# Sparse attention and mixture of experts on one core: mask products moved a step ahead, value products regrouped, GpSimd's indirect DMAs released at other places

## Chip, cores and metric

One core of a Trainium2 chip. The metric is the device time of one launch in microseconds (us). It is given as the median of several runs. A profile is one further execution, taken by the hardware profiler.

## The reference

The input is q, k and v of shape (8 batches, 8 heads, 576 positions, 64 columns), all float32. Heads 0 to 3 attend locally: position i sees positions i-31 to i. Heads 4 to 7 attend with a stride: position i sees the earlier positions that have the same remainder by 32. The outputs of all heads, laid side by side, are 4608 tokens of 512 columns. A router (a 512 by 8 product, plus a bias that depends on the token's modality) picks the best of eight experts for each token, and the token goes through that expert's two layers (512 to 1024, relu, 1024 to 512), scaled by the softmax weight of the pick:

```python
logits = x @ w_gate + modality_bias[modality_id]
e_idx = argmax(logits); gate_w = softmax(logits)[e_idx]
out[mask_e] = gate_w * (relu(x[mask_e] @ w1[e]) @ w2[e])
```

## The kernel before

**Stages.** The kernel has an attention stage and an expert stage, and TensorE (PE) runs through both without a barrier. The attention stage works in 32 *units*, two heads or two batches at a time: 16 local ones (class `Local`) and 16 strided ones (class `Strided`), alternating. Four local and four strided units make a *pair of batches*; its tokens are put in rows, routed, ranked within their expert and scattered to a list in device memory (`finish_pair`, `route`, `scatters`). The expert stage takes slots of 256 tokens from that list and runs them through `ffn`; the first slots start while the last pair of batches is still being routed.

**A unit's steps.** `load` and `load_values` issue its DMAs on the sync engine's queue (SP). `scores` adds the scores to a mask: first a *mask product*, an identity matrix (128 rows by 128 columns of PE's array) times a constant mask of 0 and -2^30, which opens the PSUM bank (L341 for the two halves of a local unit, L434 for a strided one); then many small products on top of it: eight and eight of 128 rows by 32 columns of the array (L345), four more of the same form (L352); for a strided unit 32 of 128 rows by 18 columns (L438). VectorE (DVE) takes the maximum and subtracts it, ScalarE (ACT) takes the exponential. `turn` transposes the result on PE (L208; `t` for a local unit, `ts` for a strided one) and ACT or DVE copies it to SBUF. `values` multiplies by v: a local unit has 16 products of 64 columns of the array (L390), eight into one bank and eight into another, and four of 32 columns and 64 rows (L401) between them; a strided unit has 16 of 64 columns (L482, tile `ot`). DVE then divides a local unit's rows by their sums (L406 to L408), and ACT copies a strided unit's (L490).

**What sets the order.** The order on PE is the order in which the code issues it. The loop at L1005 has one step per unit: step n issues the loads of unit n+3, the value loads of unit n-1, the scores of unit n, two pieces of leftover work (`pop(MIDS)`, pieces of `finish_pair` and `route`), `turn` of unit n-2, one `slow()`, `values` of unit n-3, three more pieces, and one more `slow()`. The order on the other engines is made by a scheduler, except where `pin` holds an instruction to the program's order. PSUM has eight banks, which all PE outputs share in turn.

**Releases.** GpSimd (POOL) issues the indirect DMAs: nine scatters of 128 token rows per pair of batches (L608), and, before the expert stage, the first weights (`raw`, L773) and tokens (`fx`, L754). Each call of `slow()` issues one of them, and `paced` makes it wait for the PE instruction that the list `recent` holds at that moment: the last transpose, or the last value product, that the code has issued. So the first `slow()` of a step waits for the transposes of `turn`, and the second for the last value product, or for a transpose that a leftover piece has put behind it.

**Setup for the router.** `routing_setup` (L227) runs once, in step 6: five small loads on SP, then two DVE instructions (L237, L239) and three GpSimd ones (L248 to L250) that make the bias of all tokens.

Of the kernel before, what the change touches and what calls it, by code (L numbers as in the profile page):

```python
# [14 lines left out]
I32 = mybir.dt.int32  # L15
# [6 lines left out]
B, H, S, D = 8, 8, 576, 64  # L22
# [4 lines left out]
DM = H * D  # L27
# [6 lines left out]
NSTATIC = 18  # L34
ROW = DM + 16
WARM = 10
SETUP = 6
POPS, MIDS, POPF = 5, 2, 2
LT, RK = 7, (10, 5)
LAG = 2  # L40
# [15 lines left out]
M_L = M_ID + P  # L56
M_S = M_L + 9 * 64
# [127 lines left out]
def attention_moe(ctx: ExitStack, tc: tile.TileContext, a, out):  # L185
    nc = tc.nc
# [6 lines left out]
    def pa(name):  # L193
        return ps.tile([P, 512], F32, tag="a", name=name)
# [10 lines left out]
    recent = []  # L205
# [21 lines left out]
    def routing_setup():  # L227

        pin(nc.sync.dma_start(wg.rearrange("p c e -> p (c e)"), a["wg"]))
        modi = cp.tile([P, 36], I32, name="modi")  # L230
        pin(nc.sync.dma_start(modi[:], a["mod"]))
        mb = cp.tile([P, 2, E], F32, name="mb_sb")
        pin(nc.sync.dma_start(mb.rearrange("p m e -> p (m e)"), a["mb"]))
        pin(nc.sync.dma_start(tok[:], a["tok"]))
        pin(nc.sync.dma_start(xd[NT:NT + 1, :], a["nul"]))
        modf = cp.tile([P, 36], F32, name="modf")
        pin(nc.vector.tensor_copy(modf[:], modi[:]))  # L237
        nmod = cp.tile([P, 36], F32, name="nmod")
        pin(nc.vector.tensor_scalar(nmod[:], modf[:], -1.0, 1.0, ALU.mult, ALU.add))  # L239
        bias0 = pools["lp"].tile([P, 36, E], F32, bufs=1, name="bias0")  # L240

        def bc_e(t):
            return t.unsqueeze(2).to_broadcast([P, 36, E])

        def bc_t(t):
            return t.unsqueeze(1).to_broadcast([P, 36, E])

        pin(nc.gpsimd.tensor_tensor(bias[:], bc_e(modf), bc_t(mb[:, 1, :]), ALU.mult))  # L248
        pin(nc.gpsimd.tensor_tensor(bias0[:], bc_e(nmod), bc_t(mb[:, 0, :]), ALU.mult))
        pin(nc.gpsimd.tensor_tensor(bias[:], bias[:], bias0[:], ALU.add))  # L250

# [62 lines left out]
    class Local:  # L314
# [10 lines left out]
        def load_values(self):  # L325
# [6 lines left out]
            if n < 2:  # L332
                pin(ins)

        def scores(self):
            n, q, kd = self.n, self.qk[:, 0, 19:37, :], self.qk[:, :, 0:19, :]
            self.ex = ex = lp.tile([P, 9, 64], F32, tag="ex", name=f"ex{n}")
            for half in range(2):
                gn = 4 + half
                sp = pa(f"s{n}{half}")[:, :64 * gn]  # L340
                nc.tensor.matmul(sp, identb, cb[:, M_L + 256 * half:M_L + 256 * half + 64 * gn], start=True, stop=True)  # L341
                for m in range(2):
                    for u in range(4):
                        i = _place(2 * half + m, u)
                        nc.tensor.matmul(  # L345
                            sp[32 * u:32 * u + 32, 128 * m:128 * m + 128], q[:, i, :], kd[:, :, i:i + 2, :],
                            start=False, stop=True, skip_group_check=True,
                        )
                if half:
                    for u in range(4):  # L350
                        i = 16 + u // 2
                        nc.tensor.matmul(  # L352
                            sp[32 * u:32 * u + 32, 256:320], q[:, i, :],
                            kd[:, u % 2, i:i + 2, :].rearrange("p i q -> p (i q)"),
                            start=False, stop=True, skip_group_check=True,
                        )
# [25 lines left out]

        def values(self):
            n, et, e8, vv, xt, h = self.n, self.et, self.e8, self.vv, self.xt, self.h
            for bb in range(2):
                gn = 5 - bb
                o = pa(f"o{n}{bb}")[:, :(D + 1) * gn].rearrange("p (g c) -> p g c", g=gn)
                for k in range(4):
                    for jj in range(2):
                        recent[:] = [nc.tensor.matmul(  # L390
                            o[64 * jj:64 * jj + 64, k, :],
                            et[:, 2 * (k // 2) + bb, 2 * (k % 2) + jj, :, :].rearrange("p g q -> p (g q)"),
                            vv[:, 4 * k + 2 * jj + bb, :],
                            start=True, stop=True, skip_group_check=True,
                        )]
                if bb == 0:
                    for jj in range(2):
                        for b2 in range(2):
                            r0 = 64 * b2 + 32 * jj
                            u = 2 * jj + b2  # L400
                            nc.tensor.matmul(  # L401
                                o[r0:r0 + 32, 4, :], e8[:, 32 * u:32 * u + 32], vv[0:64, 16 + u, :],
                                start=True, stop=True, skip_group_check=True,
                            )
                rs = lp.tile([P, 5], F32, tag="rs", name=f"rs{n}{bb}")
                nc.vector.tensor_scalar(rs[:, :gn], o[:, :, D], 1e-9, None, ALU.add)  # L406
                nc.vector.reciprocal(rs[:, :gn], rs[:, :gn])
                nc.vector.tensor_tensor(  # L408
                    xt[:, 5 * bb:5 * bb + gn, D * h:D * h + D], o[:, :, 0:D],
                    rs[:, :gn].unsqueeze(2).to_broadcast([P, gn, D]), ALU.mult,  # L410
                )

    class Strided:

# [9 lines left out]
        def load_values(self):  # L424
# [3 lines left out]
            if n < 2:  # L428
                pin(ins)

        def scores(self):
            n, qk = self.n, self.qk
            s = pa(f"ss{n}")[:, :288]
            nc.tensor.matmul(s, identb, cb[:, M_S:M_S + 288], start=True, stop=True)  # L434
            for i in range(8):
                for u in range(4):
                    r = 16 * (i // 4) + 4 * u + i % 4
                    nc.tensor.matmul(  # L438
                        s[32 * u:32 * u + 18, 36 * i:36 * i + 36], qk[:, 32 + r, :], qk[:, r:r + 65:64, :],
                        start=False, stop=True, skip_group_check=True,  # L440
                    )
            s3 = s.rearrange("p (i k) -> p i k", i=16)

            def bc(t):
# [82 lines left out]
    def route(bp, xt, xcs):  # L527
# [59 lines left out]
        nc.vector.tensor_reduce(sm[:], lo[:], AX.X, ALU.add)  # L587
        nc.vector.tensor_scalar(sm[:], sm[:], 1e-9, None, ALU.add)
        nc.gpsimd.memset(xt[:, :, DM + 2:ROW], 0.0)
        nc.vector.tensor_copy(xt[:, :, DM].bitcast(I32), tok[:, 9 * bp:9 * bp + 9])  # L590
        nc.vector.reciprocal(xt[:, :, DM + 1], sm[:])

        for _ in range(RK[bp == NBP - 1]):
# [368 lines left out]
    def slow():  # L962
        while calm and next(calm[0], calm) is calm:
            calm.pop(0)
# [3 lines left out]
    def pop(k):  # L968
        for _ in range(k):
            while extra and next(extra[0], extra) is extra:  # L970
                extra.pop(0)
# [30 lines left out]
        units[i].load()  # L1002
    man = tc.manual_schedule(engines={mybir.EngineType.PE})
    man.__enter__()
    for n in range(nu + 3):  # L1005
        if n + 3 < nu:
            units[n + 3].load()
        if 1 <= n <= nu:
            units[n - 1].load_values()
        if n < nu:  # L1010
            units[n].scores()
            pop(MIDS)
        if 2 <= n <= nu + 1:
            units[n - 2].turn()
        slow()
        if n >= 3:
            units[n - 3].values()
            if n - 3 in ends:
                extra.append(after(*ends[n - 3]))
        if n == SETUP:  # L1020
            routing_setup()
        pop(POPS - MIDS if n < nu else POPS)
        slow()
        if n == nu + 1:
            turn(0)
    while calm:
# [71 lines left out]
```

## Time and profile before

| what | value |
|---|---|
| median of 3 runs | 596.82 us (595.97 to 598.28) |
| the profiled execution | 594.6 us |
| its span, first to last instruction | 592.8 us |
| PE busy | 568.4 us, 96% of the span |
| DVE, ACT, GpSimd busy | 72%, 60%, 38% |
| HBM traffic | 241 GB/s over the span |

The times of an instruction are its start and its length. PE's products overlap, and their ends are modelled, so the time that a run of products holds PE is read from its start to the start of the next run, not from its length. A product of float32 operands shows as two records, so that eight products read "x16". "128\*32" in a PE row is the part of the array that it uses, rows by columns. A gap ahead of an instruction stands in brackets with what ended it; "issue" means that the profile shows nothing that it waited for. The DMA share is the mean busy share of the core's 16 DMA engines. In section 3 of the page, "instruction" queues are those by which the engines' own instructions are fetched.

### The profile page before, as it was taken

To read this page: it belongs to the slowest core of one execution; us is meant where nothing else is said; L and a number is where in the kernel's file an instruction comes from. 1 tells how busy PE (TensorE), PEld (TensorE's weight loads), DVE (VectorE), ACT (ScalarE), POOL (GpSimd) and SP (SyncE) were. 2 spreads that over 40 slices of the span, in tenths; PEclk is the share of its full clock that TensorE was granted. 3 is DMA by queue.
4 is the path that set the end of the run, shared out by engine and by line. 5 is a ranking of instruction groups with operands and counts; after the bars stand their busy time and mean duration, and the time that the engine had idled before them with its cause. 6 is when DMAs were issued, how large, how long until landed. Compare 5 with 4: busy or idle time off the path is not lost.

```text
span 592.8 us, 15232 instructions
## 1 busy us (share of the span) xinstructions
PE 568.4 (96%) x6040; PEld 491.0 (83%) x6040; DVE 425.2 (72%) x1082; ACT 358.5 (60%) x739; POOL 227.9 (38%) x201
## 2 busy tenths in 40 slices
PE   7888998898999999999999999999999999999995
PEld 4666776676887999999999999999998998999984
DVE  6556674957969997867867767777777777677542
ACT  3345765656866566666666666666665676666642
POOL 1010041233666786652542533533534533332310
PEclk9789999999999999999999999999999999999999
DMA  8998698996798855964934932413504438200721
GB/s 275 289 263 258 201 346 268 297 352 223 261 219 212 267 147 174 245 187 108 276 102 124 214 138 64 108 38 73 108 28 81 109 127 247 70 14 25 241 97 39
DMA packets 66670, 102.50 MB, mean 173 GB/s; under 512 B 47327, under 2 KB 48607, under 8 KB 63008
## 3 DMA queue, kind: packets, MB, share of 16 engines
q0 software_dynamic: 19744, 58.57, 29.9%
q1 hardware_dynamic: 46560, 42.48, 28.3%
q8 instruction: 49, 0.80, 0.6%
q10 hardware_dynamic: 288, 0.41, 0.3%
q14 instruction: 29, 0.24, 0.1%
HBM read 123.66 MB, written 19.43 MB: 241 GB/s over the span
## 4 chain that ended last, share of the span: by engine, by line
PE 90%; issue 5%; DVE 2%; DMA 1%; ACT 1%; POOL 0%; POOLq 0%; ACTq 0%
PE h L886 35%; PE o L900 34%; PE o L390 3%; PE s L345 3%; PE ot L482 3%; PE ss L438 2%; PE t L208 2%; PE xl L208 1%; PE ts L208 1%; PE xs L208 1%; PE s L341 1%; PE lg L533 1%; DMA lqk<-in_qkl 1%; PE o L401 1%; DMA xd<-xt,posi 1%
## 5 line engine op out<-in xcount | busy, mean ns | idle before, releaser
L922 DVE TENSOR_TENSOR wl<-raw,wh 128x512 fp32r<-128x512 f32 x288 | 186.2, 685 | 85.1 <-ACT wh L921 83.8
L921 ACT CAST wh<-raw 128x512 fp32r<-128x512 f32 x288 | 164.2, 619 | 90.6 <-PE o L900 90.5
L886 PE MATMUL h<-xl,wh 128*128 128x256 f32 x576 | 162.0, 282 | 1.1 <-DVE xl L874 1.1
L886 PE MATMUL h<-xh,wl 128*128 128x256 f32 x576 | 163.0, 284 | 0.0
L886 PE MATMUL h<-xh,wh 128*128 128x256 f32 x576 | 162.6, 284 | 0.2 <-ACT xh L873 0.2
L773 POOL DMA_INDIRECT raw<-in_w,wi x72 | 90.9, 1263 | 166.7 <-DVE wl L922 154.1
L886 PEld LDWEIGHTS h<-xl,wh 128*128 128x128 f32 x576 | 108.7, 189 | 7.6 <-DVE xl L874 1.3
L900 PE MATMUL o<-wh,hh 128*128 128x512 f32 x288 | 114.5, 398 | 0.0
L886 PEld LDWEIGHTS h<-xh,wh 128*128 128x128 f32 x576 | 108.4, 189 | 6.7 <-ACT xh L873 0.6
L900 PE MATMUL o<-wl,hh 128*128 128x512 f32 x288 | 113.6, 394 | 0.0
L900 PE MATMUL o<-wh,hl 128*128 128x512 f32 x288 | 112.3, 395 | 0.0
L886 PEld LDWEIGHTS h<-xh,wl 128*128 128x128 f32 x576 | 108.3, 188 | 0.9
L889 ACT ACTIVATE hh<-h 128x256 fp32r<-128x256 f32 x144 | 55.4, 385 | 54.7 <-PE h L886 52.7
L608 POOL DMA_INDIRECT xd<-xt,posi x36 | 40.4, 1122 | 83.9 <-DVE xt L408 50.4
L891 DVE SCALAR_TENSOR_TENSOR hl<-h,hh 128x256 fp32r<-128x256 f32 x144 | 60.1, 418 | 12.0 <-ACT hh L889 12.0
L900 PEld LDWEIGHTS o<-wh,hl 128*128 128x128 f32 x288 | 53.7, 188 | 11.7
L900 PEld LDWEIGHTS o<-wh,hh 128*128 128x128 f32 x288 | 54.3, 188 | 7.7
L900 PEld LDWEIGHTS o<-wl,hh 128*128 128x128 f32 x288 | 54.3, 189 | 5.9
L908 POOL DMA_INDIRECT out<-y,le x36 | 46.0, 1278 | 24.6 <-ACT y L907 17.4
L754 POOL DMA_INDIRECT fx<-xd,li x36 | 39.2, 1088 | 23.5 <-issue 11.9
L379 ACT COPY et<-t 64x512 f32<-64x512 f32 x32 | 18.6, 580 | 29.3 <-PE t L208 28.9
L907 ACT ACTIVATE y<-o,le 128x512 f32<-128x512 f32 x36 | 24.6, 689 | 4.3 <-PE o L900 4.2
(180 smaller groups left out, 673.1 us busy)
## 6 DMA issues: line engine op xcount, KB each, us to landing
lqk<-in_qkl SPq DMA_DIRECT2D x32, 296.0 KB
sqk<-in_qks SPq DMA_DIRECT2D x32, 288.0 KB
vv<-in_vl SPq DMA_DIRECT2D x16, 520.0 KB
vs<-in_vs SPq DMA_DIRECT2D x16, 288.0 KB
raw<-in_w,wi POOLq DMA_INDIRECT x72, 4.9
vv<-in_vl SPq DMA_DIRECT2D x16, 65.0 KB
xd<-xt,posi POOLq DMA_INDIRECT x36, 5.8
fx<-xd,li POOLq DMA_INDIRECT x36, 4.5
```

The source lines that it names most:

```text
L208: recent[:] = [nc.tensor.transpose(dst, src, ident)]
L608: scattered(bp, paced(nc.gpsimd.indirect_dma_start(xd[0:(bp + 1) * T2, :], IOA(ap=posi[:, i:i + 1], axis=0), xt[:, i, :], None)))
L754: yield xt, fetches(min(xrows // T2, NBP) - 1, nc.gpsimd.indirect_dma_start(xt[:, h, :], None, xd[0:xrows, :], IOA(ap=li[:, s, h:h + 1], a ...
L773: return nc.gpsimd.indirect_dma_start(raws[j].rearrange("p f c -> p (f c)"), None, a["w"], IOA(ap=wi[:, s, j:j + 1], axis=0), bounds_check ...
L886: recent[:] = [nc.tensor.matmul(hp, w[:, a1], x[:, c, :], start=(k == 0), stop=(k == 11))]
L889: nc.scalar.activation(hh[:], hp, AF.Relu)
L891: nc.vector.scalar_tensor_tensor(hl[:], hp, 0.0, hh.bitcast(F32), ALU.max, ALU.subtract)
L900: nc.tensor.matmul(os[h], hx[:, m], w[:, 512:1024], start=(f == 0 and i == 0), stop=(f == 7 and i == 2))
L907: nc.scalar.mul(y[:], os[h], gate[:, h:h + 1])
L908: outs.add(nc.gpsimd.indirect_dma_start(out, IOA(ap=le[:, h, 0:1], axis=0), y[:], None, bounds_check=NT - 1, oob_is_err=False))
L921: nc.scalar.copy(wh[:, c], raw[:, c])
L922: nc.vector.tensor_tensor(wl[:, c], raw[:, c], wh[:, c].bitcast(F32), ALU.subtract)
```

## The change

The change has five parts.

1. Each class has a new method `masks`, with the mask products that stood at the head of `scores`. The loop calls it one step ahead: unit 0's before the loop, unit n+1's in step n behind `turn` and the first `slow()`, ahead of `values` of unit n-3.
2. In a local unit's `values`, the eight products of the first bank come first, then the eight of the second, then the four of 32 columns, which now go to the second bank. So the first bank has 4 groups and the second 5, and the rows land where they did.
3. A strided unit's last score product is put in `recent`, and the place of a step's second `slow()` moves: in an odd step (scores of a strided unit) one `slow()` comes right behind `scores`, and the last one ahead of the leftover pieces rather than behind them; an even step has only the `slow()` behind `turn`. Two steps together still have four.
4. `routing_setup` is now in two parts: its loads stay in step 6, its arithmetic goes to step 9, and its first DVE instruction is `paced`.
5. The copy of the token numbers (L590) is `paced` as well.

```diff
-SETUP = 6
+SETUP = 6, 9
...
         pin(nc.sync.dma_start(xd[NT:NT + 1, :], a["nul"]))
+        yield
...
-        pin(nc.vector.tensor_copy(modf[:], modi[:]))
+        pin(paced(nc.vector.tensor_copy(modf[:], modi[:])))
...
+        def masks(self):
+            self.sp = []
+            for half in range(2):
+                gn = 4 + half
+                sp = pa(f"s{self.n}{half}")[:, :64 * gn]
+                nc.tensor.matmul(sp, identb, cb[:, M_L + 256 * half:M_L + 256 * half + 64 * gn], start=True, stop=True)
+                self.sp.append(sp)
...
-            for half in range(2):
+            for half, sp in enumerate(self.sp):
...
+            blocks(0)
+            normed(0)
+            blocks(1)
+            ends()
+            normed(1)
...
+        def masks(self):
+            self.s = pa(f"ss{self.n}")[:, :288]
+            nc.tensor.matmul(self.s, identb, cb[:, M_S:M_S + 288], start=True, stop=True)
...
-                    nc.tensor.matmul(
+                    recent[:] = [nc.tensor.matmul(
                         s[32 * u:32 * u + 18, 36 * i:36 * i + 36], qk[:, 32 + r, :], qk[:, r:r + 65:64, :],
...
-        nc.vector.tensor_copy(xt[:, :, DM].bitcast(I32), tok[:, 9 * bp:9 * bp + 9])
+        paced(nc.vector.tensor_copy(xt[:, :, DM].bitcast(I32), tok[:, 9 * bp:9 * bp + 9]))
...
+    units[0].masks()
+    setup = routing_setup()
     for n in range(nu + 3):
...
             units[n].scores()
+            if n % 2:
+                slow()
             pop(MIDS)
         if 2 <= n <= nu + 1:
             units[n - 2].turn()
         slow()
+        if n + 1 < nu:
+            units[n + 1].masks()
         if n >= 3:
             units[n - 3].values()
             if n - 3 in ends:
                 extra.append(after(*ends[n - 3]))
-        if n == SETUP:
-            routing_setup()
+        if n in SETUP:
+            next(setup)
+        if n >= nu or n % 2:
+            slow()
         pop(POPS - MIDS if n < nu else POPS)
-        slow()
```

**The order on PE, local half of two steps.** Before, from the transposes of a strided unit (`ts2`) through the value products of a local unit (`o20`, `o21`: its two banks) to the scores of the next local unit (`s40`, `s41`: its two halves):

```order
L208 MATMUL ts2_661<-cf_sb_65,ens2_486 72x128 x4
L390 MATMUL o20_670<-vv2_440,et0_88 64x65 x8
L401 MATMUL o20_670<-vv2_440,e82_574 32x65 x4
L390 MATMUL o21_687<-vv2_440,et0_88 64x65 x8
L341 LDWEIGHTS cb_sb_63
L341 MATMUL s40_705<-cb_sb_63 128x256
L345 MATMUL s40_705<-lqk0_84 32x128 x8
L341 LDWEIGHTS cb_sb_63
L341 MATMUL s41_719<-cb_sb_63 128x320
L345 MATMUL s41_719<-lqk0_84 32x128 x8
L352 MATMUL s41_719<-lqk0_84 32x64 x4
```

The same place now (the line numbers are those of the changed file: L342 is the mask, L398 and L410 the value products, L353 and L360 the scores):

```order
L208 MATMUL ts2_653<-cf_sb_65,ens2_486 72x128 x4
L342 LDWEIGHTS cb_sb_63
L342 MATMUL s40_662<-cb_sb_63 128x256
L342 LDWEIGHTS cb_sb_63
L342 MATMUL s41_664<-cb_sb_63 128x320
L398 MATMUL o20_666<-vv2_442,et0_88 64x65 x8
L398 MATMUL o21_667<-vv2_442,et0_88 64x65 x8
L410 MATMUL o21_667<-vv2_442,e82_574 32x65 x4
L353 MATMUL s40_662<-lqk0_84 32x128 x8
L353 MATMUL s41_664<-lqk0_84 32x128 x8
L360 MATMUL s41_664<-lqk0_84 32x64 x4
```

The two masks stand together behind the transposes, the value products run 64, 64, 32 columns rather than 64, 32, 64, and the two halves of the scores follow each other with nothing between.

**The order on PE, strided half.** Before, from the transposes of a local unit (`t13`, `t23`) through the value products of a strided unit (`ot20`, `ot21`) to a strided unit's scores (`ss4`):

```order
L208 MATMUL t13_738<-cf_sb_65,ex3_531 128x128 x4
L208 MATMUL t23_743<-cf_sb_65,ex3_531 64x128
L482 MATMUL ot20_749<-eb2_666,vs2_529 64x72 x8
L482 MATMUL ot21_759<-eb2_666,vs2_529 64x72 x8
L434 LDWEIGHTS cb_sb_63
L434 MATMUL ss4_774<-cb_sb_63 128x288
L438 MATMUL ss4_774<-sqk0_86 18x36 x32
```

Now (L451 is the mask, L502 the value products, L458 the scores):

```order
L208 MATMUL t13_730<-cf_sb_65,ex3_535 128x128 x4
L208 MATMUL t23_735<-cf_sb_65,ex3_535 64x128
L451 LDWEIGHTS cb_sb_63
L451 MATMUL ss4_741<-cb_sb_63 128x288
L502 MATMUL ot20_743<-eb2_658,vs2_533 64x72 x8
L502 MATMUL ot21_753<-eb2_658,vs2_533 64x72 x8
L458 MATMUL ss4_741<-sqk0_86 18x36 x32
```

The strided mask has moved ahead of the value products, to the transposes. The order on SP is the same row for row. On GpSimd it is the same but for one place: of the nine scatters of the third pair of batches, six rather than five now stand ahead of the third and fourth weight loads (`raw`). What changes there is the PE instruction that a DMA waits for: where that was the last product of `ot`, it is now, in the steps of the first 32 units, the last strided score.

More of the change, by code (lines that the diff above doesn't have):

```diff
@@ L250, in routing_setup @@
         pin(nc.gpsimd.tensor_tensor(bias[:], bias[:], bias0[:], ALU.add))
+        yield
     cnt = cp.tile([P, NBP + 1, E], BF16, name="cnt")
@@ L337, in scores @@
             self.ex = ex = lp.tile([P, 9, 64], F32, tag="ex", name=f"ex{n}")
-            for half in range(2):
+            for half, sp in enumerate(self.sp):
                 gn = 4 + half
-                sp = pa(f"s{n}{half}")[:, :64 * gn]
-                nc.tensor.matmul(sp, identb, cb[:, M_L + 256 * half:M_L + 256 * half + 64 * gn], start=True, stop=True)
                 for m in range(2):
@@ L384, in values, with blocks @@
             n, et, e8, vv, xt, h = self.n, self.et, self.e8, self.vv, self.xt, self.h
-            for bb in range(2):
-                gn = 5 - bb
-                o = pa(f"o{n}{bb}")[:, :(D + 1) * gn].rearrange("p (g c) -> p g c", g=gn)
+            os = [pa(f"o{n}{bb}")[:, :(D + 1) * (4 + bb)].rearrange("p (g c) -> p g c", g=4 + bb) for bb in range(2)]
+            def blocks(bb):
                 for k in range(4):
@@ L390, in values @@
                         recent[:] = [nc.tensor.matmul(
-                            o[64 * jj:64 * jj + 64, k, :],
+                            os[bb][64 * jj:64 * jj + 64, bb + k, :],
                             et[:, 2 * (k // 2) + bb, 2 * (k % 2) + jj, :, :].rearrange("p g q -> p (g q)"),
@@ L395, in values, with ends, normed @@
                         )]
[L396 to L404, printed above, removed]
+            def ends():
+                for jj in range(2):
+                    for b2 in range(2):
+                        r0 = 64 * b2 + 32 * jj
+                        u = 2 * jj + b2
+                        nc.tensor.matmul(
+                            os[1][r0:r0 + 32, 0, :], e8[:, 32 * u:32 * u + 32], vv[0:64, 16 + u, :],
+                            start=True, stop=True, skip_group_check=True,
+                        )
+            def normed(bb):
+                o, gn = os[bb], 4 + bb
                 rs = lp.tile([P, 5], F32, tag="rs", name=f"rs{n}{bb}")
@@ L408, in values @@
                 nc.vector.tensor_tensor(
-                    xt[:, 5 * bb:5 * bb + gn, D * h:D * h + D], o[:, :, 0:D],
+                    xt[:, 4 * bb:4 * bb + gn, D * h:D * h + D], o[:, :, 0:D],
                     rs[:, :gn].unsqueeze(2).to_broadcast([P, gn, D]), ALU.mult,
                 )
+            blocks(0)
[3 more added lines that the diff above has]
+            normed(1)
     class Strided:
@@ L429, in load_values @@
                 pin(ins)
+        def masks(self):
+            self.s = pa(f"ss{self.n}")[:, :288]
+            nc.tensor.matmul(self.s, identb, cb[:, M_S:M_S + 288], start=True, stop=True)
         def scores(self):
-            n, qk = self.n, self.qk
-            s = pa(f"ss{n}")[:, :288]
-            nc.tensor.matmul(s, identb, cb[:, M_S:M_S + 288], start=True, stop=True)
+            n, qk, s = self.n, self.qk, self.s
             for i in range(8):
@@ L437, in scores @@
                     r = 16 * (i // 4) + 4 * u + i % 4
-                    nc.tensor.matmul(
+                    recent[:] = [nc.tensor.matmul(
                         s[32 * u:32 * u + 18, 36 * i:36 * i + 36], qk[:, 32 + r, :], qk[:, r:r + 65:64, :],
                         start=False, stop=True, skip_group_check=True,
-                    )
+                    )]
             s3 = s.rearrange("p (i k) -> p i k", i=16)
```

## Prediction

> **What bounds the kernel now.** The page comes first: which engine is full.
>
> ```profile
> span 592.8 us, 15232 instructions
> ...
> PE 568.4 (96%) x6040; PEld 491.0 (83%) x6040; DVE 425.2 (72%) x1082; ACT 358.5 (60%) x739; POOL 227.9 (38%) x201
> ```
>
> PE is. The busy time by stretches then tells where it is not: up to 56 us, to the start of the expert stage at 157 us, and from there on.
>
> ```profile
> core 0: us, PE busy (x) PEld busy (x) DVE busy (x) ACT busy (x) POOL busy (x), PEclk, DMA share, GB/s
> 6.70:56.00 49.30, 40.91 (x1015) 30.62 (x1017) 30.01 (x96) 22.99 (x54) 2.11 (x3) 0.90 0.93 277
> 56.00:157.00 101.00, 94.67 (x2262) 73.38 (x2261) 72.29 (x326) 65.28 (x153) 28.13 (x31) 1.00 0.83 280
> 157.00:593.00 436.00, 428.11 (x2759) 385.50 (x2756) 318.56 (x654) 268.90 (x534) 194.97 (x158) 1.00 0.49 136
> ```
>
> The expert stage is PE's from end to end (428.11 of 436 us, the rest is the tail), and the change touches nothing in it. So all that the change can win or lose lies in the attention stage, 150.3 us, of which PE is idle for 8.4 + 6.3 = 14.7 us; whatever that stage gains, the end gains. The view of PE's waits says what those are:
>
> ```profile
> PE ss L438 <- issue: 4.0, 3, 1.8
> PE s L345 <- issue: 3.9, 3, 2.1
> PE o L401 <- issue: 2.3, 2, 1.3
> ...
> PE ct L654 <- DVE cnt L584: 1.8, 2, 1.1
> ...
> PE ot L482 <- issue: 0.7, 1, 0.7
> PE xs L208 <- DVE xt L408: 0.4, 1, 0.4
> ```
>
> Four "issue" rows hold nine waits and 10.9 us. They wait for no semaphore: in the timeline they fall in the middle of a run of like products, here in front of the ninth record of sixteen and of the sixth of eight.
>
> ```profile
> 29.12 0.43 PE L345 MATMUL s<-lqk 128*32 128x128 f32 x8 [2.06 <-issue]
> ...
> 90.68 0.30 PE L401 MATMUL o<-vv,e 64*32 64x65 f32 x3 [1.25 <-issue]
> ```
>
> The DMA view from 6 to 157 us has a queue that carries instructions:
>
> ```profile
> q8 instruction: 26, 0.43, 1.2%
> ```
>
> 26 packets for 1015 + 1017 + 2262 + 2261 = 6555 PE records: one packet (0.43 MB / 26 = 16.5 KB) per 252. I read the nine waits as PE running out of instructions: its next packet stands among the loads in DMA engines that are 83 to 93% busy. That is a reading; no row names the releaser.
>
> **Term 1: changes of the array's shape, a gain.** Two steps in steady state, as the timeline has them:
>
> ```profile
> 66.17 0.60 PE L208 MATMUL ts<-cf_sb,ens 128*72 128x128 f32 x4
> 66.70 0.69 PE L390 MATMUL o<-vv,et 128*64 128x65 f32 x16
> 67.31 0.32 PE L401 MATMUL o<-vv,e 64*32 64x65 f32 x8
> 67.56 0.69 PE L390 MATMUL o<-vv,et 128*64 128x65 f32 x16
> 68.18 0.28 PE L341 MATMUL s<-cb_sb 128*128 128x256 bf16 x1
> 68.39 0.64 PE L345 MATMUL s<-lqk 128*32 128x128 f32 x16
> 68.97 0.31 PE L341 MATMUL s<-cb_sb 128*128 128x320 bf16 x1
> 69.21 0.65 PE L345 MATMUL s<-lqk 128*32 128x128 f32 x16
> 69.67 0.29 PE L352 MATMUL s<-lqk 128*32 128x64 f32 x8
> 69.89 0.77 PE L208 MATMUL t<-cf_sb,ex 128*128 128x128 f32 x5
> 70.59 1.22 PE L482 MATMUL ot<-eb,vs 72*64 72x72 f32 x32
> 71.74 0.30 PE L434 MATMUL ss<-cb_sb 128*128 128x288 bf16 x1
> 71.97 0.75 PE L438 MATMUL ss<-sqk 128*18 128x36 f32 x64
> 72.65 0.21 PE L599 MATMUL rk<-ohb,cb_sb 128*128 128x72 bf16 x1
> 72.69 0.20 PE L600 MATMUL rk<-cum,cb_sb 128*128 128x72 bf16 x1
> 72.73 0.60 PE L208 MATMUL ts<-cf_sb,ens 128*72 128x128 f32 x4
> ```
>
> The same sixteen records of L345 hold PE for 68.97 - 68.39 = 0.58 us when a mask follows and for 69.67 - 69.21 = 0.46 us when L352, of the same shape, does. So a change of shape costs about 0.12 us. L599, L600 and the transposes behind them, all of the full array, follow at 0.04 us, bf16 or float32: a mask next to transposes costs no change. Counted down these rows (transposes of 72 columns and masks use the array's full width, scores of 18 columns are like those of 32), a pair of steps changes shape 12 times: into L390, L401, L390, mask, L345, mask, L345, `t`, `ot`, mask, L438, `ts`. The new order has 7: into L390, L401, the scores, `t`, `ot`, L438, `ts`. Five fewer are 0.6 us per pair of steps, 16 x 0.6 = 9.6 us. From below: if values gain nothing from being joined, four fewer, 7.7 us; from above, with 0.13 each, 10.4 us. No work is added: every product is still there.
>
> **Term 2: what the instruction packets take back, a loss.** Where a block of 252 records ended in a wait, the packet's arrival sets the end of the block, and faster products only lengthen the wait. 9 of 26 blocks did: 9.6 x 9/26 = 3.3 us. A block shortened by 0.37 us brings the next packet into view sooner; no row shows how near the other 17 are, so the bounds are none and all 17 (6.3 us more), and I take three, 1.1 us, as a shortening of 0.37 us in blocks of 150.3 / 26 = 5.8 us is small. Loss 4.4 us.
>
> By the Trainium skill's page "Runtime: NRT & Kernel Launch", section "Instruction fetch mechanics", instructions come in blocks of 256 while the block before is executed, and a block's crossing is "mostly hidden". The block size agrees with 252 records a packet; hidden it is not here, by the 10.9 us above. By that rule this loss would be zero, and that is a rival below.
>
> **Term 3: DVE sets two places, a loss.** In the routing of pairs 1 and 2 PE waits for `cnt` (1.8 us in two waits). Ahead of the first one:
>
> ```profile
> 102.20:109.40 7.20, 6.54 (x190) 4.97 (x188) 7.16 (x37) 4.45 (x11) 0.00 (x0) 1.00 0.79 244
> ```
>
> DVE works 7.16 of 7.20 us there, so a PE that is 0.6 us sooner waits 0.6 us longer: 2 x 0.6 = 1.2 us lost. (None, if DVE begins as much sooner; 2.4 if pair 0 is caught too and the joined `values` make it worse.)
>
> **Term 4: where GpSimd's DMAs run, a gain.**
>
> ```profile
> 78.53 1.12 PE L438 MATMUL ss<-sqk 128*18 128x36 f32 x64
> ...
> 86.34 1.10 PE L438 MATMUL ss<-sqk 128*18 128x36 f32 x64
> ...
> 136.89 1.04 PE L438 MATMUL ss<-sqk 128*18 128x36 f32 x64
> ```
>
> ```profile
> 78.77 0.96 POOL L608 DMA_INDIRECT xd<-xt,posi  x1 [0.30 <-PE ot L482]
> ```
>
> Five of the sixteen strided scores, of which these are the first two and the last, take 1.04 to 1.12 us rather than 0.75. In the first GpSimd starts a scatter, released by `ot`, 0.24 us in. The change releases that one behind the scores: at most 5 x 0.37 = 1.8 us. But 86.34 lies in the block that ends with the wait at 90.68, and whatever a block with a wait saves is lost, as in term 2. I take 0.4 us; the lower bound is zero. The section "SBUF: two separate sides" of the skill's "SBUF — State Buffer" says that compute and DMA cannot slow each other and that PE's reads never wait; by it the slow scores had another cause and this term is zero. The coincidence speaks for the term; one run cannot settle it.
>
> **Term 5: the last scatter of a pair.** It waited for a piece behind `lg`:
>
> ```profile
> 95.72 0.96 POOL L608 DMA_INDIRECT xd<-xt,posi  x1 [5.90 <-ACT xt L499]
> ```
>
> It now goes behind the values at about 92 us, and the wait of `xs` for `xt` (0.4 us, above) can go; zero to 0.4, I take 0.2.
>
> **Edits that I cost at nothing.** The paced copy of `modf` and of `tok` stands, on DVE, behind rows that already read later PE output, so its wait is over; queued behind are the maxima of the next scores. The three bias instructions (2.11 us of POOL in the first stretch) move from step 6 to 9, long before the first scatter at 76 us. One more scatter (0.96 + 0.30 = 1.26 us) now stands on POOL ahead of
>
> ```profile
> 157.77 1.04 POOL L773 DMA_INDIRECT raw<-in_w,wi  x1 [0.30 <-issue]
> ```
>
> the weights of the fifth part of the first slot; four parts of 2.84 us, with routing between, run first. SP's order is the same; its loads follow the buffers that PE frees, and go with it. The masks hold their banks for a step longer:
>
> ```profile
> 70.64 1.19 ACT L379 COPY et<-t 64x512 f32<-64x512 f32 x2 [1.42 <-PE t L208]
> ```
>
> The second mask now opens, behind `ts` (72.73 + 0.53 = 73.3 us), the bank that these copies have left at 71.83: 1.4 us to spare.
>
> **Sum.** -9.6 + 4.4 + 1.2 - 0.4 - 0.2 = -4.6 us. The profiled execution took 594.6 us, 592.8 of it span; it would take 590.0. The median shown, 596.82, lies 2.2 us above it, so I forecast 592.2.
>
> **Rivals.**
> *Fetch hidden.* The wait belongs to something that goes with PE, or packets come sooner with fewer scatters in the way; term 2 and DVE's excess vanish and term 4 counts in full: -9.6 + 1.2 - 1.8 - 0.4 = -10.6, 586.2 us. For it: 17 of 26 packets cause no wait. Against: waits in mid-run. The page cited in term 2 says this. 0.13.
> *Gain absorbed.* DMA engines at 0.93 and 0.83 are asked for the same bytes sooner, every packet is as much later, and all blocks wait: -9.6 + 9.6 + 0, less the 0.6 of terms 4 and 5, with part of term 3: 595.8 us. 0.25.
> *Slower: banks.* Eight banks turn over, and three masks per pair of steps now hold theirs from before `values`. It decides once ACT or DVE leaves a bank more than 1.4 us later than above; in the routing steps ACT has copies of 0.6 us more (1.19 / 2). One copy late in each of 16 local steps is 16 x 0.6 = 9.6: 592.2 + 9.6 = 601.8 us. Against: ACT is busy 65% of the second stretch. 0.10.
> *Releases do nothing.* Scores stay slow with a scatter elsewhere: 592.6 us. 0.05.
> The forecast has 0.47, its own range 589.5 to 594.5 from the bounds of terms 1, 2 and 4.
>
> **Numbers.** About 0.5%, 3 us, is what this kernel's runs (0.4% apart) can tell. Below 593.8: fetch hidden, most of the forecast and of the fourth rival, 0.59. Above 599.8: banks and a corner, 0.11. Between: 0.30. The range leaves out banks and the lower half of fetch hidden: 586.5 to 597.5.
>
> **What would show it.** Right: L345's halves one run of about 0.9 us; L390 one of about 1.1; strided scores all near 0.75; "issue" waits as many or more, 11 to 15 us; `ct` near 3 us; expert stage beginning at about 152 us. Wrong: "issue" waits gone (fetch hidden), or PE waiting at L342 or L451 for ACT or DVE (banks), or start of experts at 156 or later.

## The result, and the profile after

The changed kernel took 602.06 us (median of 22 runs), the kernel before 597.18 us beside it; the ratio is 1.0057, 95% interval 1.0035 to 1.0080. It is slower, where 592.2 us was forecast, and outside the range. The experiments come from four later jobs, each with its own runs of the kernel before: it took 597.9 us in one of them and 607 to 608 us in three, and one chip gave both kinds. What sets this the runs do not show; every ratio below is against the runs of before in the same job. The medians are of all runs, while a ratio leaves out the runs that took over 1.5% more than the fastest of their kernel, so the two can differ.

The profiled execution of the changed kernel took 598.35 us. Its page, first lines:

```profile
span 596.6 us, 15228 instructions
...
PE 562.2 (94%) x6040; PEld 493.7 (83%) x6040; DVE 424.4 (71%) x1082; ACT 358.4 (60%) x739; POOL 224.3 (38%) x201
```

PE is busy for 6.2 us less (568.4 before), and the span is 3.8 us longer (592.8 before). The two steps of the prediction's first listing, as the timeline of the changed kernel has them:

```profile
64.42 0.75 PE L458 MATMUL ss<-sqk 128*18 128x36 f32 x64
...
65.92 0.41 PE L342 MATMUL s<-cb_sb 128*128 128x256 bf16 x2
66.26 1.15 PE L398 MATMUL o<-vv,et 128*64 128x65 f32 x32
67.35 0.32 PE L410 MATMUL o<-vv,e 64*32 64x65 f32 x8
67.59 1.08 PE L353 MATMUL s<-lqk 128*32 128x128 f32 x32
68.49 0.29 PE L360 MATMUL s<-lqk 128*32 128x64 f32 x8
68.72 0.77 PE L208 MATMUL t<-cf_sb,ex 128*128 128x128 f32 x5
69.32 0.29 PE L451 MATMUL ss<-cb_sb 128*128 128x288 bf16 x1
69.53 1.22 PE L502 MATMUL ot<-eb,vs 72*64 72x72 f32 x32
70.69 0.75 PE L458 MATMUL ss<-sqk 128*18 128x36 f32 x64
```

The local scores (67.59 to 68.72) are one run, the values (66.26 to 67.59) too, and from the local scores to the strided ones it is 70.69 - 67.59 = 3.10 us, where it was 71.97 - 68.39 = 3.58 us before. The strided scores one pair of steps earlier stand in the trace of before at

```profile
65.10 0.75 PE L438 MATMUL ss<-sqk 128*18 128x36 f32 x64
```

From strided scores to strided scores it is 6.27 us now (64.42 to 70.69), where it was 6.87 (65.10 to 71.97): 0.6 us per pair of steps, as forecast. Now the view of PE's waits:

```profile
PE ss L458 <- issue: 6.9, 5, 3.3
PE s L353 <- issue: 4.2, 3, 2.0
PE ot L502 <- issue: 3.2, 2, 1.9
PE o L398 <- issue: 2.6, 2, 1.7
...
PE ct L674 <- DVE cnt L604: 1.6, 2, 1.3
PE o L410 <- issue: 1.4, 1, 1.4
PE h L906 <- DVE xl L894: 1.4, 1, 1.4
PE ot L502 <- ACT et L387: 1.1, 1, 1.1
...
PE h L906 <- ACT xh L893: 0.9, 1, 0.9
PE ct L674 <- ACT xc L510: 0.8, 1, 0.8
```

The "issue" waits are 13 and 18.3 us, where nine and 10.9 us stood before. That they are waits at instruction packets, which the prediction called a reading, the two traces can settle. If every PE record is counted (matmuls, weight loads and those of its sequencer), 450 records stand ahead of the first of the waits in both traces, and ahead of each of the others a whole multiple of 256 more, give or take one: 706, 962, 1217, up to 6082. So these waits stand only where a block of 256 records ends. The packets come no sooner than before: the 23rd lands at 143.2 us, where it was 141.7.

And by stretches, cut at the start of the expert stage, now 158 us:

```profile
core 0: us, PE busy (x) PEld busy (x) DVE busy (x) ACT busy (x) POOL busy (x), PEclk, DMA share, GB/s
6.70:56.00 49.30, 37.67 (x1021) 30.59 (x1020) 30.12 (x96) 23.43 (x54) 2.25 (x3) 0.90 0.93 278
56.00:158.00 102.00, 89.98 (x2256) 74.19 (x2253) 70.87 (x326) 65.17 (x153) 28.11 (x31) 0.98 0.84 276
158.00:597.00 439.00, 429.75 (x2759) 387.31 (x2756) 319.06 (x655) 268.56 (x534) 191.25 (x158) 0.99 0.49 135
```

The last two rows differ from those of before in PEclk: the granted clock, 1.00 in both later stretches before, is 0.98 and 0.99. The trace's clock records show why the mean is not 1: in some windows of 3.41 us it is exactly 0.5. Three such windows stand in either profile between 14 and 42 us; the changed one has two more, at 126.55 and at 191.4 us. Four windows in a row:

```profile
119.73:123.14 3.41, 3.41 (x82) 2.85 (x72) 3.38 (x13) 2.33 (x6) 1.68 (x2) 1.00 1.03 360
123.14:126.55 3.41, 1.40 (x70) 1.22 (x63) 0.52 (x3) 1.89 (x5) 0.29 (x1) 1.00 1.01 401
126.55:129.96 3.41, 3.41 (x44) 2.68 (x45) 2.06 (x7) 1.81 (x4) 1.63 (x2) 0.50 0.99 270
129.96:133.37 3.41, 3.41 (x57) 2.23 (x57) 0.63 (x3) 1.07 (x3) 0.96 (x1) 1.00 0.99 354
```

PE stands still for 2.01 us of the second window, and in the third, fully busy, its clock is halved. The timeline of the same place shows both, the wait and what it costs behind it:

```profile
125.38 0.59 PE L458 MATMUL ss<-sqk 128*18 128x36 f32 x46 [2.01 <-issue]
...
127.93 2.00 PE L398 MATMUL o<-vv,et 128*64 128x65 f32 x32
```

The 32 value records take 2.00 us, not 1.15. So a wait can cost twice: once as a wait, and again, up to 1.7 us, in the window behind it.

The following table splits the time from 6.0 us to the first expert product, by the records of each trace. Waits at packets are waits without a semaphore that end 1.1 to 1.7 us after an instruction packet has landed; short ones are the others without a semaphore (a few of them may fall among the first by chance). Half clock is half of the time in halved windows, waits in them left out. That is the most that it can cost, since products that something else bounds lose less; so work, which is the rest, is a lower figure.

| profile | to experts | work | packets | semaphores | short | half clock |
|---|---|---|---|---|---|---|
| before, first comparison | 151.2 | 131.4 | 10.9 | 3.7 | 0.3 | 4.9 |
| changed, first comparison | 152.2 | 122.6 | 18.3 | 5.3 | 0.0 | 5.9 |
| before, job at 607.9 | 159.6 | 132.4 | 9.6 | 8.4 | 5.5 | 3.8 |
| changed, job at 607.9 | 155.0 | 125.0 | 13.7 | 5.9 | 1.5 | 8.9 |
| before, job at 597.9 | 153.0 | 129.5 | 11.7 | 6.7 | 0.2 | 4.9 |
| changed, job at 597.9 | 154.4 | 122.6 | 14.9 | 6.5 | 0.5 | 9.9 |

In the first comparison 8.8 us of work went and 8.7 us of waits came (7.4 at packets, 1.6 behind semaphores, less 0.3), and 1.0 us by the clock: the experts begin 1.0 us later. The other 2.8 us are lost in the expert stage: its first waits grew from 1.2 to 2.6 us (the two L906 rows above and 0.3 us in one of L674), and the window behind them, at 191.4 us, is halved.

In the two later pairs less went to the packets (4.1 and 3.2 us) and more to the clock (up to 5.1 and 5.0 us). The profile of the first comparison is also not its typical run: its mean clock is 0.984, and that of the 22 runs of the changed kernel 0.976. The clocks of the runs of before are not on record there, so how much of the 0.57% is the clock stays open.

### The profile page after: what moved, and what is told of

The parts are those of the page before. It is cut to its first block, busy times and chain, and to the rows that moved or that the text cites. A ratio compares the mean times of both kernels' runs of the same rounds, so it can differ in the third digit from the quotient of the medians.

```text
span 596.6 us, 15228 instructions
## 1 busy us (share of the span) xinstructions
PE 562.2 (94%) x6040; PEld 493.7 (83%) x6040; DVE 424.4 (71%) x1082; ACT 358.4 (60%) x739; POOL 224.3 (38%) x201
## 4 chain that ended last, share of the span: by engine, by line
PE 87%; issue 5%; DVE 3%; DMA 2%; ACT 1%; POOL 0%; SPq 0%; POOLq 0%; ACTq 0%
PE h L906 34%; PE o L920 32%; PE o L398 3%; PE ot L502 3%; PE s L353 3%; PE xl L208 2%; PE xs L208 2%; PE t L208 2%; PE ss L458 2%; PE ts L208 1%; PE lg L553 1%; DMA vv<-in_vl 1%; DVE wl L942 1%; PE warm L307 1%; PE o L410 1%
## 5 line engine op out<-in xcount | busy, mean ns | idle before, releaser
L906 PE MATMUL h<-xh,wh 128*128 128x256 f32 x576 | 163.7, 285 | 0.9 <-ACT xh L893 0.9
L906 PE MATMUL h<-xl,wh 128*128 128x256 f32 x576 | 162.9, 284 | 1.4 <-DVE xl L894 1.4
L906 PE MATMUL h<-xh,wl 128*128 128x256 f32 x576 | 164.0, 285 | 0.0
L906 PEld LDWEIGHTS h<-xl,wh 128*128 128x128 f32 x576 | 109.6, 191 | 7.9 <-DVE xl L894 1.6
L906 PEld LDWEIGHTS h<-xh,wh 128*128 128x128 f32 x576 | 109.5, 190 | 7.4 <-ACT xh L893 1.3
L906 PEld LDWEIGHTS h<-xh,wl 128*128 128x128 f32 x576 | 109.2, 190 | 0.9
L911 DVE SCALAR_TENSOR_TENSOR hl<-h,hh 128x256 fp32r<-128x256 f32 x144 | 60.4, 420 | 13.5 <-ACT hh L909 13.4
L628 POOL DMA_INDIRECT xd<-xt,posi x36 | 37.7, 1047 | 70.9 <-ACT exs L474 24.2
```

Source lines behind the costliest of these rows:

```text
L628: scattered(bp, paced(nc.gpsimd.indirect_dma_start(xd[0:(bp + 1) * T2, :], IOA(ap=posi[:, i:i + 1], axis=0), xt[:, i, :], None)))
L906: recent[:] = [nc.tensor.matmul(hp, w[:, a1], x[:, c, :], start=(k == 0), stop=(k == 11))]
L911: nc.vector.scalar_tensor_tensor(hl[:], hp, 0.0, hh.bitcast(F32), ALU.max, ALU.subtract)
```

## The experiments

**Theory and rivals.** F: the faster products run into the instruction packets, which come no sooner. C: the clock makes the loss, since PE is granted less of it. R: the new release places of GpSimd's DMAs make it.

**One part at a time.** Four kernels in one job (before 606.75 us, 35 runs). The masks alone:

```diff
+    units[0].masks()
...
+        if n + 1 < nu:
+            units[n + 1].masks()
```

> Before, with the mask products a step ahead and nothing else changed: 8 changes of array shape per pair of steps rather than 12, 4 x 0.12 x 16 = 7.7 us less work for PE. Theory F (the faster products are given back as longer waits at the ends of instruction packets): the time is within 0.4% of before, the issue waits grow from 10.9 us by 4 to 8 us. Rival C (the clock: a denser PE is granted less): waits as before, mean granted clock lower by 0.005 or more, time 0 to 0.7% over before. Rival R (the new release places of GpSimd's DMAs make the loss): faster than before by 0.7 to 1.3%.

Measured: 610.48 us, ratio 1.0022 (0.9989 to 1.0056). The values alone (64, 64, 32 columns; masks where they were):

> Before, with the 32-column value products last and nothing else changed: one change of shape fewer, 1 x 0.12 x 16 = 1.9 us. All theories: within 0.4% of before, F at 0 to 0.2% less. If it is slower by over 0.5%, the joined value products hold a copy or a bank, and none of the three is the cause.

Measured: 606.59 us, 0.9999 (0.9971 to 1.0027). The release places, with the paced copies and the setup in two parts, alone:

```diff
+            if n % 2:
+                slow()
             pop(MIDS)
...
+        if n >= nu or n % 2:
+            slow()
         pop(POPS - MIDS if n < nu else POPS)
-        slow()
```

> Before, with the new release places, the two paced copies and the bias in step 9, but masks and values as they were: no change of shape is saved. Theory F: within 0.4% of before, issue waits 9 to 13 us. Rival C: the same time and clock as before. Rival R: slower than before by 0.6% or more (what the whole change loses, 3.4 us, and what it should have won besides), with issue waits of 14 us or more.

Measured: 602.82 us, 0.9925 (0.9894 to 0.9955): faster. Masks and values without the release places:

> The changed kernel with the old release places, without the paced copies and with the whole setup in step 6: masks and values are the new ones, 5 changes fewer per pair, 9.6 us. Theory F: as the changed kernel, 0.2 to 0.9% over before, issue waits 15 to 20 us. Rival C: 0.2 to 0.9% over before with a clock lower by 0.005 or more and issue waits near 11 us. Rival R: faster than before by 0.7% or more.

Measured: 609.35 us, 1.0034 (1.0007 to 1.0062). So R falls: the release places win here, and masks and values, which save the work, win nothing. F has missed its sign: with masks and values together the "issue" waits are 13.4 us, not 15 to 20, and those at packets about 8 us. With the masks alone they are 17.7 us, as F had it, but only about 12 of them at packets. C has its sign: the masks' runs had a mean clock of 0.975, those of before 0.981, those with the release places alone 0.985, and 0.006 of 605 us is 3.6 us. Split as in the table, half clock is up to 14.8 us with the masks alone, 16.0 with masks and values, 8.5 with the release places alone. The kernel before was not profiled in this job, so the shares of waits and clock in the loss are not shown. What lowers the clock is left to the wait by itself, below.

**The same job, with and without loads.** Next, in a job at 607.9 us, the two kernels as they are, and both with the loads left out, so that all later units compute on the data of the first two of their class:

```diff
-            load_qk(self.qk...)
+            if n < 2:
+                load_qk(self.qk...)
...
+            if n >= 2:
+                self.vv = held["vv", n % 2]
+                return
```

> The kernel before once more, for its trace on the chip on which the next kernels run. Theory G (PE waits for its instruction packets; a wait of about 1 us within one 3.4-us window halves the granted clock for the next window, which loses up to 1.7 us more): as many half-clock windows as the granted clock says, each behind a window with 0.9 us or more of PE waiting. Rival S (what differs between the kernels is work, not waiting): waits and half-clock windows as in the changed kernel.

> The changed kernel beside the kernel before on the same chip. Theory G: 0.2 to 0.9% slower, with a mean granted clock lower by 0.003 to 0.008 (2 to 5 us) than that of the runs of before. Rival S: slower with the same clock.

> The kernel before with only the first two units' q, k and v of each class loaded; all later units compute on those. This takes some 30 MB of loads out of the attention stage. Theory G: the packets arrive at once, issue waits under 3 us (from 10.9) and no half-clock window between 20 and 150 us; the expert stage begins 12 to 20 us sooner (waits of 10 us and clock losses of 5 us and the first loads' waits). Rival S, or if the waits belong to PE itself: issue waits stay at 8 us or more.

> The changed kernel with the same loads left out. Theory G: with nothing to wait for, the five saved changes of shape per pair of steps come through: the expert stage begins 8 to 10.5 us sooner than in the kernel before with the same loads left out, and the time is lower by as much. Rival S (the new order costs as much work as it saves, by banks, copies or joined products): no difference, or slower.

Measured: before 606.54 us in one run; the changed kernel 602.80 us, ratio 0.9924 (0.9881 to 0.9966), faster here and not slower as expected; without loads the kernel before 597.73 us (0.9854, 0.9776 to 0.9932) and the changed one 585.44 us (0.9652, 0.9592 to 0.9713). Without loads the changed kernel is 12.3 us the faster, and its experts begin at 142.75 us, against 159.74 us, which is more than the 8 to 10.5 us expected. Waits at packets fall to one each, of 2.8 us at 16.35 us (before) and 2.1 us at 14.44 us (changed), behind the first loads; half clock in the attention stage is 4.8 and 1.4 us, short waits 6.3 and 2.4 us, work 131.8 and 123.3 us. So 8.5 of the 17.0 us are work, and the rest is mainly clock and short waits. For the kernel before the expectation was missed: its experts begin 5.9 us sooner than with loads (165.62 us), not 12 to 20, its short waits stay, and one window is halved at 143.33 us. The changed kernel by stretches, without loads:

```profile
20.00:56.00 36.00, 36.00 (x1007) 30.12 (x1003) 26.94 (x92) 26.49 (x63) 2.26 (x3) 1.00 0.02 4
56.00:142.00 86.00, 78.63 (x1989) 63.66 (x1979) 65.67 (x305) 55.19 (x131) 29.20 (x32) 1.00 0.31 113
```

From 20 to 56 us PE never stops, at a DMA share of 0.02. A packet starts, by the median, 0.2 to 0.8 us after the block before its own is begun in the three profiles without loads, and 2.2 to 3.2 us after it in the other 15. This shows that the packets' waits come from the loads, and that the saved work is real. The Trainium skill ("Runtime: NRT & Kernel Launch", section "Instruction fetch mechanics") calls the crossing of a block mostly hidden: with the DMA engines at 0.02 to 0.31 that agrees, at 0.83 to 0.93 it does not (10.9 to 18.3 us).

But the sign had turned against the first comparison. The kernel before, in this job, at the place of the prediction's term 4; PE first, then GpSimd:

```profile
79.28 0.39 PE L438 MATMUL ss<-sqk 128*18 128x36 f32 x22
79.99 0.53 PE L438 MATMUL ss<-sqk 128*18 128x36 f32 x28 [0.33 <-issue]
80.97 0.23 PE L438 MATMUL ss<-sqk 128*18 128x36 f32 x3 [0.45 <-issue]
81.70 0.34 PE L438 MATMUL ss<-sqk 128*18 128x36 f32 x11 [0.49 <-issue]
```

```profile
78.66 0.96 POOL L608 DMA_INDIRECT xd<-xt,posi  x1 [0.76 <-PE ot L482]
80.35 0.96 POOL L608 DMA_INDIRECT xd<-xt,posi  x1 [0.73 <-PE ot L482]
```

The strided scores, 1.12 us in the first profile, take 2.7 us here, with three stops that no packet explains, beside two scatters. The waits in strided scores in this profile, and in that of the release places alone in the job before, on another chip:

```profile
PE ss L438 <- issue: 11.9, 16, 3.5
```

```profile
PE ss L440 <- issue: 2.9, 5, 1.2
```

16 waits in strided scores (three of them at packets) stand against five. The changed kernel, with the new release places, has 4 us less of short stops than before in this job (1.5 and 5.5 us in the table); in the first comparison there were next to none to take away (0.3 us).

**Which of the two a job is.** Theory H: the release places are worth what the scatters' stops cost in that job.

> The changed kernel once more, since it was 0.6% slower than the kernel before in the first comparison and 0.8% faster in the second, on another chip. Theory H (chips differ in whether a scatter stops PE while GpSimd writes it: where it does, the changed release places win back some 4 us and more): 0.5 to 1.1% faster where the trace shows short issue waits of 0.2 to 0.5 us outside the ends of packets in number, 0.3 to 0.9% slower where it shows none. Rival N (the two results are noise of one effect near zero): within 0.3%.

Measured, in a third job at 607.6 us: 603.33 us, 0.9915 (0.9883 to 0.9947). Before was not profiled there, so that scatters stopped PE in that job too is not shown. Then the parts once more, in one job, which came out at 597.91 us (25 runs of before):

> The kernel before, for its trace on this chip. Theory H (the chips differ in whether a scatter stops PE): at about 597 us there are few short waits in strided scores beside scatters (under 1 us in all), at about 607 us there are 4 us or more of them.

> The changed kernel. Theory H: 0.3 to 0.9% slower than before if before takes about 597 us on this chip, 0.5 to 1.1% faster if it takes about 607 us. Rival N (noise): within 0.3% either way.

> The kernel before with the new release places alone. Theory H: within 0.4% of before if before takes about 597 us, 0.4 to 1.1% faster if it takes about 607 us.

> The changed masks and values with the old release places. Theory H: 0.2 to 0.9% slower than before on either kind of chip; then the whole change is the sum of the two parts. Rival A (the parts do not add up, the masks need the release places to win): slower by over 0.3% where the whole change wins.

Measured: before 596.76 us in one run, with 0.2 us of short stops in all; the changed kernel 598.79 us, 0.9996 (0.9948 to 1.0044); the release places alone 596.71 us, 0.9980 (0.9929 to 1.0031); masks and values 600.56 us, 1.0029 (0.9983 to 1.0074). H fits in part. The traces agree with it: the stops stand in the profiles of two jobs at 607 to 608 us, and all but missing (0.5 us or less in all) from those of the two at 597 to 598 us. The release places are worth 0.75% in the one kind and too little to tell in the other, and masks and values come out 0.3% over before in both (here within the interval). But the intervals of the release places overlap (0.9894 to 0.9955, 0.9929 to 1.0031), and the changed kernel came out level here, where H expected it 0.3 to 0.9% slower; that is what the rival of noise expected. Noise is not all of it, since the changed kernel's two results of 0.99 have intervals that do not reach 1. The first comparison's 1.0057 and this job's 0.9996 have intervals that overlap (1.0035 to 1.0044); the runs of one kernel scatter with the clock: the 25 of before lie between 594.5 us (clock 0.985) and 608.9 us (0.961).

**A wait by itself.** Is it the wait that halves the clock, or the products that run? In the changed kernel without loads, eight steps hold the next masks behind four DVE instructions, which start behind the step's transposes:

```diff
+        for _ in range(4):
+            last = pin(paced(nc.vector.tensor_tensor(lull[:], ...)))
...
+            lulled[:] = [paced_hold(n)] if n in range(8, 32, 3) else []
             units[n + 1].masks()
```

> The changed kernel with the loads of later units left out, and in eight steps (every third from 8 to 29) the next unit's masks wait for four DVE instructions that start behind the step's transposes, so that PE stands still for about 2 us each. Theory C (a wait of PE of about 1 us or more in one 3.4-us window halves the granted clock in the next): four to eight half-clock windows between 50 and 150 us where the kernel without the waits has none, and the expert stage begins later by the waits and 1 to 1.7 us more for each half-clock window. Rival: the halved clock comes from something else (which products run, the loads): no new half-clock window, and later by the waits alone.

Measured: 626.75 us. The waits, and two windows behind one of them (its wait ended at 72.94 us and was 4.18 us long):

```profile
PE ss L470 <- DVE lull L323: 12.9, 4, 4.2
PE s L359 <- DVE lull L323: 12.3, 4, 3.5
```

```profile
69.40:72.82 3.42, 0.00 (x0) 0.00 (x0) 3.42 (x17) 1.68 (x4) 0.00 (x0) 1.00 0.00 0
72.82:76.23 3.41, 3.29 (x89) 2.90 (x93) 0.07 (x1) 1.32 (x2) 0.00 (x0) 0.50 0.02 5
76.23:79.64 3.41, 3.41 (x60) 2.69 (x50) 2.92 (x11) 1.33 (x3) 0.00 (x0) 0.50 0.01 2
```

Seven of the eight waits (2.5 to 4.2 us) halved the next window, five of them the one after it too: 12 halved windows, where the kernel without these waits had none between 20 and 142 us. The eighth, the shortest, fell across the edge of two windows, with 1.3 and 1.2 us in them, and no halved window followed. (Two more halved windows, from 178.64 us on, stand behind short stops.) The experts begin 42.8 us later; waits are 24.0 us more, half clock up to 22.7 us more. The waits make the halved clock, though this was one run on another chip than the kernel without them. The four to eight windows expected were too few, since a second often follows.

**Loads spread out.** If packets queue behind bursts of loads, spreading the loads should help:

```diff
-            units[n + 3].load()
-            units[n - 1].load_values()
+        pieces = chain(units[n + 3].load(), units[n - 1].load_values())
+        next(pieces, None)
...
+        tc.add_manual_dep(ins.ins, mark[0].ins.name, ...)
```

> The changed kernel with its loads spread over a step: of the loads that stood together at a step's start, the second half of q and k goes behind the scores, the first half of v behind the transposes, the rest of v behind the value products. The same bytes. Theory G (a packet of instructions queues behind the burst of loads): waits at the ends of packets fall from 14 to 18 us to under 9 us, fewer half-clock windows, the time 5 to 12 us under the changed kernel's. Rival B (the DMA engines are simply full at 0.83 to 0.93, and order does not matter): waits and time as in the changed kernel, within 3 us. Rival L: the loads come late and PE waits for lqk, sqk, vv or vs, slower.

> The kernel before with the new release places (as in the run of the release places alone) and the loads spread as in the run before this one. Theory G: faster than the release places alone by 2 to 8 us, and slower than the changed kernel with spread loads by 3 to 9 us, since its 9.6 us of shape changes are then worth having. Rival B: as the release places alone, 0.9925 of before.

Measured: 619.57 us (1.0162, 1.0097 to 1.0228) and 618.96 us (1.0150, 1.0089 to 1.0211): both slower, where both were expected to be faster: a miss for the theory in this form. The first stretch of the changed kernel in that job, with its loads as they are, and with them spread:

```profile
6.50:56.00 49.50, 36.74 (x1020) 30.07 (x1020) 29.69 (x95) 23.34 (x54) 2.25 (x3) 0.93 0.95 281
```

```profile
6.50:56.00 49.50, 34.02 (x963) 27.84 (x963) 27.98 (x90) 21.62 (x50) 2.24 (x3) 0.93 0.97 252
```

Spread, the engines were as busy (0.97) and moved less (252 GB/s against 281), and waits at packets grew from 16.5 to 22.1 us. The median start of a packet did not come sooner (3.0 us after the block before its own is begun, 2.9 with the loads as they are). The loads themselves came late too, as a rival had it: PE waited 7.5 us for `vs`, `lqk` and `vv`, against 1.8. So spreading in this form does not help. As it cost throughput, it does not show whether a burst by itself makes a packet late; and the cut of v into two loads and the waits on PE came together here, so which of them cost the throughput is open.

The best version tried is the kernel before with the release places alone: 0.9925 of before in one job, 0.9980, which is no difference, in the other. Beside the changed kernel it stood only in the second, at 596.71 against 598.79 us, within the scatter of both.

## Why the prediction was wrong

Two steps failed: term 2 was too small, and the clock, a cost of the waits, was put at nothing. Between them they took back about all that term 1 won: 8.4, 9.2 and 8.2 us (the clock's part at its most) in the table's three pairs, against 8.8, 7.4 and 6.9 us of work.

- *Term 1, changes of shape, -9.6 us: right.* The steady pair saves 0.60 us, a pair with routing products among its steps 0.50 us (5.15 + 3.29 against 4.77 + 3.17), so 8.0 to 9.6 us over 16 pairs, inside the bounds. The work in the table fell by 6.9 to 8.8 us, without loads by 8.5 us.
- *Term 2, packets, +4.4 us: the first step that failed.* It charged the nine blocks that had waits and three of the other 17. In the first comparison the packets took back 7.4 us, in 13 waits. The prediction said that no row showed how near the other blocks were; the trace of before does show it. The nine blocks begin 1.27 to 1.52 us after their packet has landed, and seven of the 17 begin 1.25 to 1.82 us after theirs, so with about half a us to spare or none. Charged for 16 blocks, the term would have been 9.6 x 16/26 = 5.9 us. In the two later pairs the packets took 4.1 and 3.2 us, near the 4.4; there the size was right. The rival "gain absorbed" had the mechanism right, but not all blocks wait, and its 595.8 us has no clock in it either.
- *Left out: the clock, the second step that failed.* The 0.90 in the row of the first stretch was quoted and not asked about. Longer waits halve the clock behind them: up to 1.0, 5.1 and 5.0 us in the attention stage of the three pairs.
- *"Whatever that stage gains, the end gains":* not so. In the first comparison the waits in the expert stage grew by 1.4 us, and the window halved behind them costs up to 1.7 us; the stage took 2.8 us more. In that profile this turned a gain absorbed into a loss.
- *Term 3, `ct` behind DVE, +1.2 us:* the two waits are 1.3 and 0.8 us, the second behind ACT's `xc`, 2.0 us in all against 1.8, so +0.2 (the 0.3 us left in the view's row for `cnt` stand in the expert stage).
- *Term 4, scatters beside scores, -0.4 us:* right in mechanism. Of the five strided scores that took 1.04 to 1.12 us, three take 0.75 us now, and the other two have a packet's wait in them. In the job at 607.9 us, where scatters stop PE altogether, the short stops fell by 4 us, and there the change came out a gain. The Trainium skill's "SBUF — State Buffer", section "SBUF: two separate sides", would have it at zero; these rows do not agree, though what a stopped PE waits for no row names.
- *Term 5, `xs` behind `xt`, -0.2 us:* its wait of 0.4 us is gone in this profile; in another job's it stands at 0.5 us.
- *Banks, the rival on the slow side:* it came at most once, not 16 times (L502 behind `et`, 1.1 us). That its 601.8 us lies beside the 602.06 measured is chance.

Of what should have been seen, the joined runs came, and three of the five slow strided scores at 0.75 us; `ct` near 3 us was 2.4 with all its rows, "issue" waits of 11 to 15 us were 18.3, and experts at 152 us were at 158.2.

## What to carry to other kernels

Where the engine waits for instructions or loads that other traffic sets, work taken off it returns as waiting: before counting a gain, ask for each block of instructions how long its packet has been there when it is needed. The trace tells it, as the time from the landing of the packet to the block's first record. On this chip a wait of PE is then not only its own length: in a window with 1.5 us of it or more, add up to 1.7 us for the next window. Measure in more than one job before a change of half a per cent is believed.

## What the runs showed of the hardware

- **The clock's windows.** In the 18 profiles, 80 halved windows of 3.41 us follow one at full clock. In every one of those 80 PE had stood still for 0.93 us or more. With 1.5 us or more, 59 of 66 windows were followed by a halved one; with 2.0 us or more, all 31. The Trainium skill ("TensorE: Matmul & The Clock Gate", section "Part 1: The HAM clock gate") has the clock fall to half after an idle window of about 3.4 us; the windows and the halving agree, the idle time does not: here 2 us in a window were always enough.
- **Stops beside scatters.** While GpSimd issues a scatter, or just behind it, small products stop for 0.2 to 0.5 us, mostly twice or so per run of strided scores, in two of the jobs at 607 to 608 us; in the jobs at 597 to 598 us, one of them on a chip that showed the stops earlier, the same products only slow down (1.04 to 1.12 us for 0.75).
- **Instruction packets.** One packet serves 256 PE records. It takes about 1.1 us (median 1.0 to 1.2 us, with loads and without). Where PE waited for one, it went on 1.3 to 1.6 us after the landing in the first two profiles.
